# Pooled attention and a softplus feed-forward layer: other addresses for the tiles that TensorE reads

## The chip, the cores and the metric

The kernel runs on one core of a Trainium2 chip. The metric is the device time of one execution in microseconds (us), as the median of several runs. A profile, taken by the hardware profiler in one further execution, shows what each engine of the core did: PE is TensorE's matmuls, PEld its loads of the stationary operand, DVE is VectorE, ACT ScalarE, POOL GpSimd and SP the queue that issues the DMAs.

## The reference

Eight batches, eight heads, 576 positions, a head dimension of 64. Keys and values are averaged over groups of 8 positions, so there are 72 of each; the attention's result, as 4608 tokens of 512, goes through a feed-forward layer with 2048 inner columns and softplus between its two products.

```
k_p = k.reshape(B, H, 72, 8, D).mean(axis=3)
v_p = v.reshape(B, H, 72, 8, D).mean(axis=3)
scores = matmul(q, k_p.T) / sqrt(D);  scores -= max(scores)
attn = exp(scores) / (sum(exp(scores)) + 1e-9)
x = matmul(attn, v_p)                  # then to 4608 x 512
h = x @ w_in                           # 512 x 2048
g = maximum(h, 0) + log1p(exp(-abs(h)))
out = g @ w_out                        # 2048 x 512
```

## The kernel before, in words

The tokens are cut into 18 chunks of 256 (`CT`), each of two tiles of 128. For a chunk the kernel makes `x`, the attention's result with the 512 columns on the partitions, and then `h` in 16 blocks `f` of 128 inner columns, two blocks making a pair `u`. Each matrix is split into a high and a low part of float32r, and a product of two matrices is three products (high by high, low by high, high by low).

**First product** (`ffn1_products`, line 488): the stationary operand, which PE loads, is a 128x128 piece of the weights `w`; the moving operand, which PE streams past it, is a piece of `x` of 256 columns. A block `f` takes 12 matmuls, a pair 24.

**Second product.** In the first four chunks (lines 510 and 570) the stationary operand is a piece of `g` and the moving one a row of 512 weights, into `acc`. From the fifth chunk on (line 678, `pair2_fast`) a scheme of seven products on quarters takes the place of eight: the stationary operand is a 128x128 piece of `gh`, `gl` or of `so` (sums of pieces of g), and the moving one 256 columns of the weights, 21 matmuls a pair, into `m`. So `w` is the stationary operand on line 488 and the moving one on line 678.

**Attention** stands between these groups in short groups of its own on PE: `qTp` (transposes of q, line 331), `sc` (scores, 351), `ptp` and `ltp` (transposes of the normalised exponentials `pm` and `pe`, 414 and 426), `avp` (attention by values, 455 and 462) and `kT` (213). VectorE makes the lowest score `mn`, the sum `sm`, `pm`, `pe`, the low parts and the sums; ScalarE makes the exponentials, softplus and the high parts.

**What sets the order.** Every operation is given to a planner (`Order`) with a cost in us, the operations it follows and the kinds of tile slots it needs; the planner lists the operations by the start that it works out, and they are issued in that order. None of its costs, slots or kinds is touched.

**Where tiles lie.** A pool hands out addresses in SBUF (bytes within a partition) in the order in which its tags first appear, and pools lie one behind the other in the order in which they are opened: `const`, `wpool` (the weights, 16 tiles of 8192 bytes and what the early stretch uses for raw weights), then `one` (all else). The address modulo 256 bytes is called the phase here. All tiles that PE reads in the two products are multiples of 256 bytes long, so a tile's phase is set by what stands ahead of it in its pool and by the pools ahead of that, among them small tiles such as `mn` (32 bytes), `sm` (32 bytes) and `pe` (112 elements, of which 96 are used).

Of the kernel before, what the change touches and what calls it, by code (L numbers as in the profile page):

```python
# [9 lines left out]
F32 = mybir.dt.float32  # L10
F32R = mybir.dt.float32r
# [92 lines left out]
def pooled_attention_softplus_ffn(  # L104
# [11 lines left out]
    B, H, S, D = q.shape  # L116
    NTOK, DM = out.shape
    DFF = w_in.shape[1]
    P = 128
# [5 lines left out]
    CT = T * P  # L125
    HP = H // 2
# [3 lines left out]
    N1 = 3  # L130
# [4 lines left out]

    PSUM = bass.MemoryType.PSUM
    const = ctx.enter_context(tc.tile_pool(name="const", bufs=1))
    wpool = ctx.enter_context(tc.tile_pool(name="wpool", bufs=1))
    one = ctx.enter_context(tc.tile_pool(name="one", bufs=1))
    psum = ctx.enter_context(tc.tile_pool(name="psum", bufs=1, space=PSUM))  # L140
    dram = ctx.enter_context(tc.tile_pool(name="dram", bufs=1, space=bass.MemoryType.DRAM))
# [149 lines left out]
    R = 4 * KL  # L291
# [19 lines left out]
    def new_x(c, name=None):  # L311

        if c == N1 - 1:
            x_[c] = [one.tile([P, HP, CT], F32R, tag=tag, name="x") for tag in ("Sa", "Sb")]
        else:
            x = one.tile([P, 2, HP, CT], F32R, tag={"a": "X01", "b": "X23"}[name or "ab"[c % N1]],
                         name="x")
            x_[c] = [x[:, 0], x[:, 1]]

# [3 lines left out]
    class Tile:  # L323
# [30 lines left out]
        def least(self, j, ps, tag):  # L354

            if j == 0:
                self.mn = one.tile([P, 2, HP], F32, tag="mn" + tag, name="mn")
            nc.vector.tensor_reduce(out=self.mn[:, j], in_=self.view(ps), axis=AX.X, op=ALU.min)  # L358

        def view(self, ps):  # L360
# [9 lines left out]

        def exp_sum(self, j, ps, tag):
            if j == 0:
                self.sm = one.tile([P, H], F32, tag="sm" + tag, name="sm")
            for m in range(HP):
                h = 4 * (m // 2) + 2 * j + m % 2
                nc.scalar.activation(out=e_[self.c][:, self.t, h], in_=self.view(ps)[:, m],  # L376
                                     func=AF.Exp, scale=-1.0, bias=self.mn[:, j, m:m + 1],
                                     accum_out=self.sm[:, h:h + 1])

        def sum(self, tag):  # L380
            self.sm = one.tile([P, H], F32, tag="sm" + tag, name="sm")
            nc.vector.tensor_reduce(out=self.sm, in_=e_[self.c][:, self.t], axis=AX.X, op=ALU.add)

        def reciprocal(self):
# [7 lines left out]
                                    in1=self.sm.unsqueeze(2).to_broadcast([P, H, KM]), op=ALU.mult)  # L392

        def ends(self):

            pe = one.tile([P, 6 * R + 16], F32, tag="pe", name="pe")
            self.pe = pe[:, 0:6 * R].rearrange("p (a n r) -> p a n r", a=2, n=3)
            for a in range(2):
                hs = slice(4 * a, 4 * a + 4)
                nc.vector.tensor_tensor(  # L400
                    out=self.pe[:, a].rearrange("p n (h j) -> p n h j", h=4),
                    in0=e_[self.c][:, self.t, hs, KM:SP].unsqueeze(1).to_broadcast([P, 3, 4, KL]),
                    in1=self.sm[:, hs].unsqueeze(1).unsqueeze(3).to_broadcast([P, 3, 4, KL]),
                    op=ALU.mult)
# [61 lines left out]
    def av_high(c, r, ps, name=None):  # L466
        if c not in x_:
            new_x(c, name)
        nc.scalar.copy(out=x_[c][0][:, r::2], in_=ps.rearrange("p (g i) -> p g i", g=2))
# [475 lines left out]
    def attend(c):  # L945
# [17 lines left out]
        for t, x in enumerate(tiles):  # L963
# [7 lines left out]
            q_free[c, t] = o  # L971
            o = op(ACT, act(512), lambda x=x, s=s_q, n=s_qT: x.qT_out(s.tile, n.name), [o], [s_q, s_qT])
            ends, ss = [], [Slot("bank"), Slot("bank")]
            p = op(PE, 0.7, lambda x=x, ss=ss: x.scores([bank(s, "sc") for s in ss]), [o, *keys],
                   [s_qT, *ss])
            score_done.setdefault(c, []).append(p)
            for i, s in enumerate(ss):
                d = op(DVE, 0.46, lambda x=x, i=i, s=s, n=s_mn: x.least(i, s.tile, n.name), [p, *ends],
                       [s, s_mn])
                if c < N1:  # L980
                    def exp_sum(x=x, i=i, s=s, e=s_E[0], t=t, n=s_sm):
                        if c == 0 and 0 not in e_:
                            new_E(0)
                        e_[c] = e_[0]
                        x.slot = e.name
                        x.exp_sum(i, s.tile, n.name)
                    ends.append(op(ACT, 1.2, exp_sum, [d], [s, s_mn, s_sm, *s_E], table="exp"))
                else:
                    def less(x=x, i=i, s=s):
                        if c not in e_:  # L990
                            new_E(c)
                        x.less(i, s.tile)
                    ends.append(op(DVE, 0.46, less, [d, *e_free], [s, s_mn]))
            if c < N1:
                exps.extend(ends)
            else:
                subs += ends
            norms.append((x, ends, s_E, s_sm, s_pm, s_pe))
        if c == N1:
            ex = op(ACT, 1.2, lambda: exponential(e_[c]), subs, table="exp")  # L1000
# [403 lines left out]
```

## Time and profile before

| | us |
|---|---|
| median of three runs | 904.15 |
| lowest and highest | 903.52, 904.78 |
| the profiled execution | 903.13 |
| its span, first to last instruction | 901.4 |
| PE busy (98% of the span) | 883.9 |
| PEld busy (93%) | 840.9 |
| DVE busy (72%) | 648.7 |
| ACT busy (45%) | 407.5 |

The mean granted clock of TensorE is 0.999 of full speed. Of the chain of waits, followed back from the last instruction, 95% lies on PE: line 488 has 44% of the span, line 678 has 31%, the early second products 10%. In the profile's rows `m<-w,gh` means that the instruction writes m and reads w and gh; a piece of the chain is given with its start, its length and how many instructions of one line it joins. The pieces of the chain are worked out from starts and ends, so the length of a piece is the time until the next group of matmuls begins.

### The profile page before, as it was taken

The page shows a single profiled execution, that of the slowest core. Times are in us where ns is not written, and L with a number is a line of the kernel's source. Part 1 is how long each engine was busy: PE and PEld are TensorE (multiplying, and loading weights), DVE is VectorE, ACT ScalarE, POOL GpSimd, SP SyncE. Part 2 cuts the span into 40 slices and gives each one's busy share as a digit, 9 for nine tenths or more (in the row PEclk, how much of TensorE's full clock was granted, in tenths as well). Part 3 has the DMA queues.
Part 4 walks back from the last instruction along what each step waited for, and adds up shares of the span by engine and source line. Part 5 has one row for each costly group of instructions (what it writes and reads, how often), then busy time and mean ns, then how long its engine had stood idle before and what let it go on. Part 6 is the DMA issues. An engine that isn't in the chain of part 4 may idle for free.

```text
span 901.4 us, 20496 instructions
## 1 busy us (share of the span) xinstructions
PE 883.9 (98%) x8304; PEld 840.9 (93%) x8304; DVE 648.7 (72%) x1600; ACT 407.5 (45%) x824; POOL 2.4 (0%) x19
## 2 busy tenths in 40 slices
PE   5999999999999999999999999999999999999997
PEld 3689999889999999999999999999999999999997
DVE  5899999878767678787767666776576565657454
ACT  5864443354353534443444444353545353434332
POOL 1000000000000000000000000000000000000000
PEclk9999999999999999999999999999999999999999
DMA  9976544545997788787669765877566565656472
GB/s 233 312 227 202 173 162 158 161 153 200 299 267 240 231 239 245 214 249 228 227 200 261 217 227 168 257 239 228 193 179 228 177 222 187 212 162 225 163 241 76
DMA packets 107085, 191.12 MB, mean 212 GB/s; under 512 B 46064, under 2 KB 60400, under 8 KB 106992
## 3 DMA queue, kind: packets, MB, share of 16 engines
q1 hardware_dynamic: 106992, 189.82, 68.2%
q8 instruction: 65, 1.06, 0.5%
q14 instruction: 28, 0.23, 0.1%
HBM read 167.25 MB, written 22.54 MB: 211 GB/s over the span
## 4 chain that ended last, share of the span: by engine, by line
PE 95%; DVE 2%; DMA 1%; SPq 1%; ACT 1%; issue 0%; DVEq 0%; ACTq 0%
PE h L488 44%; PE m L678 31%; PE acc L510 7%; PE acc L570 3%; PE sc L351 2%; PE avp L455 2%; PE qTp L331 2%; PE ptp L414 2%; PE avp L462 1%; DMA wst<-in_moe_w_out_dram 1%; PE ltp L426 1%; DMA kvl<-in_v_dram 1%; ACT E L376 0%; SPq L302 0%; DVE o L699 0%
## 5 line engine op out<-in xcount | busy, mean ns | idle before, releaser
L488 PE MATMUL h<-x,w 128*128 128x256 f32 x3456 | 428.7, 280 | 0.2 <-ACT g L493 0.2
L488 PEld LDWEIGHTS h<-x,w 128*128 128x128 f32 x3456 | 413.3, 188 | 4.2 <-ACT g L493 0.6
L537 ACT ACTIVATE g<-h 128x512 f32<-128x512 f32 x120 | 71.9, 599 | 280.3 <-PE h L488 277.7
L678 PE MATMUL m<-w,so 128*128 128x256 f32 x1344 | 173.9, 278 | 0.0
L678 PEld LDWEIGHTS m<-w,so 128*128 128x128 f32 x1344 | 163.8, 188 | 0.0
L678 PE MATMUL m<-w,gh 128*128 128x256 f32 x672 | 131.6, 285 | 0.0
L588 DVE TENSOR_TENSOR sf<-g 128x128 f32<-128x128 f32 x112 | 32.7, 292 | 130.1 <-ACT g L537 129.6
L678 PEld LDWEIGHTS m<-w,gh 128*128 128x128 f32 x672 | 102.1, 188 | 1.7
L602 ACT CAST so<-sf 128x512 fp32r<-128x512 f32 x112 | 69.7, 622 | 58.1 <-DVE sf L591 57.6
L607 DVE TENSOR_TENSOR so<-sf,so 128x512 fp32r<-128x512 f32 x112 | 77.3, 690 | 22.8 <-ACT so L602 22.7
L678 PE MATMUL m<-w,gl 128*128 128x256 f32 x336 | 93.5, 278 | 0.0
L558 DVE TENSOR_TENSOR gl<-g,gh 128x384 fp32r<-128x384 f32 (+1 forms) x120 | 67.2, 560 | 0.5 <-ACT gh L551 0.3
L678 PEld LDWEIGHTS m<-w,gl 128*128 128x128 f32 x336 | 63.0, 188 | 0.0
L510 PE MATMUL acc<-w,g 128*128 128x512 f32 x192 | 60.1, 394 | 0.0
L551 ACT ACTIVATE gh<-h 128x384 fp32r<-128x384 f32 (+1 forms) x120 | 59.2, 493 | 0.0
L493 ACT ACTIVATE g<-h 128x256 fp32r<-128x256 f32 x96 | 32.1, 383 | 56.6 <-PE h L488 34.3
L699 DVE TENSOR_TENSOR o<-o,m 128x256 f32<-128x256 f32 x98 | 39.7, 417 | 3.5 <-ACT o L691 0.6
L510 PEld LDWEIGHTS acc<-w,g 128*128 128x128 f32 x192 | 33.5, 188 | 5.2
L510 PE MATMUL acc<-w,gl 128*128 128x512 f32 x96 | 37.9, 395 | 0.2 <-DVE gl L499 0.2
L591 DVE TENSOR_TENSOR sf<-g,sf 128x128 f32<-128x128 f32 x112 | 32.7, 292 | 3.9
L358 DVE TENSOR_REDUCE mn<-sc 128x4 f32<-128x288 f32 x72 | 31.3, 450 | 5.5 <-PE sc L351 5.4
L400 DVE TENSOR_TENSOR pe<-E,sm 128x96 f32<-128x96 f32 x72 | 15.2, 252 | 27.7 <-PE ltp L426 27.7
(165 smaller groups left out, 925.8 us busy)
## 6 DMA issues: line engine op xcount, KB each, us to landing
w<-wi SPq DMA_DIRECT2D x224, 512.0 KB
out_dram<-o SPq DMA_DIRECT2D x36, 256.0 KB
q<-in_q_dram SPq DMA_DIRECT2D x32, 256.0 KB
wst<-in_moe_w_in_dram SPq DMA_DIRECT2D x32, 256.0 KB
wst<-in_moe_w_out_dram SPq DMA_DIRECT2D x16, 512.0 KB
wi<-w SPq DMA_DIRECT2D x16, 512.0 KB
kst<-in_k_dram SPq DMA_DIRECT2D x24, 288.0 KB
vst<-in_v_dram SPq DMA_DIRECT2D x24, 256.0 KB
```

The source lines that it names most:

```text
L488: nc.tensor.matmul(out=ps[:, 0:CT], lhsT=row(w, kc), rhs=x[:, kc], start=first and kc == j == 0, stop=last and kc == KC - 1 and j == 2)
L493: nc.scalar.activation(out=g, in_=ps[:, 0:CT], func=AF.Softplus)
L510: nc.tensor.matmul(out=accs[c][t], lhsT=a[:, ts], rhs=w, start=f == 0 and j == 0, stop=f == FC - 1 and j == 2)
L537: nc.scalar.activation(out=g, in_=x.rearrange("p (b i) -> p b i", i=P), func=AF.Softplus)
L551: nc.scalar.activation(out=gh, in_=quarters(c, x.rearrange("p (b i) -> p b i", i=P)), func=AF.Softplus)
L558: nc.vector.tensor_tensor(out=gl, in0=quarters(c, g), in1=gh.bitcast(F32), op=ALU.subtract)
L588: tt(out=sf[:, 2], in0=g[:, 0], in1=g[:, 2], op=ALU.add)
L591: tt(out=sf[:, 3], in0=g[:, 3], in1=sf[:, 1], op=ALU.subtract)
L602: nc.scalar.copy(out=so[:, 0], in_=ss[c, u])
L607: nc.vector.tensor_tensor(out=so[:, 1], in0=sf, in1=so[:, 0].bitcast(F32), op=ALU.subtract)
L678: nc.tensor.matmul(out=ms[c][n], lhsT=x, rhs=y, start=u == 0 and j == 0 and n in (1, 6, 5, 4), stop=u == FP - 1 and j == 2 and n in (2, 7, ...
L699: nc.vector.tensor_tensor(out=o, in0=in0, in1=m[n], op=how)
```

## The change

Three pools are added. `x` of the chunks (but the third, c = 2, whose `x` has the tags `Sa` and `Sb` in `one`) goes into `xpool`, and `mn` into `mpool`; both are opened ahead of the weights' pool. `sm` goes into `spool`, between `wpool` and `one`. The tile `pe` loses its 16 unused elements (64 bytes).

```
+    xpool = ctx.enter_context(tc.tile_pool(name="xpool", bufs=1))
+    mpool = ctx.enter_context(tc.tile_pool(name="mpool", bufs=1))
     wpool = ctx.enter_context(tc.tile_pool(name="wpool", bufs=1))
+    spool = ctx.enter_context(tc.tile_pool(name="spool", bufs=1))
     one = ctx.enter_context(tc.tile_pool(name="one", bufs=1))
@@ new_x
-            x = one.tile([P, 2, HP, CT], F32R, tag={"a": "X01", "b": "X23"}[name or "ab"[c % N1]],
+            x = xpool.tile([P, 2, HP, CT], F32R, tag={"a": "X01", "b": "X23"}[name or "ab"[c % N1]],
                          name="x")
@@ least
-                self.mn = one.tile([P, 2, HP], F32, tag="mn" + tag, name="mn")
+                self.mn = mpool.tile([P, 2, HP], F32, tag="mn" + tag, name="mn")
@@ exp_sum
-                self.sm = one.tile([P, H], F32, tag="sm" + tag, name="sm")
+                self.sm = spool.tile([P, H], F32, tag="sm" + tag, name="sm")
@@ sum
-            self.sm = one.tile([P, H], F32, tag="sm" + tag, name="sm")
+            self.sm = spool.tile([P, H], F32, tag="sm" + tag, name="sm")
@@ ends
-            pe = one.tile([P, 6 * R + 16], F32, tag="pe", name="pe")
-            self.pe = pe[:, 0:6 * R].rearrange("p (a n r) -> p a n r", a=2, n=3)
+            self.pe = one.tile([P, 2, 3, R], F32, tag="pe", name="pe")
```

No instruction is added, removed or moved: on each of the five engines the instructions stand in the same order in both programs, with the same waits; only addresses differ. The phases (address modulo 256) of what PE reads, as the two programs lay the tiles out, are these:

| tile | before | after |
|---|---|---|
| `w`, the weights in all their slots | 192 | 0 |
| `x` (X01, X23) | 128 | 192 |
| `x` of c = 2 (Sa, Sb) | 128 | 64 |
| `g`, `gh`, `gl`, `so`, `pm` | 128 (slot G0 of `g`: 64) | 64 (G0 too) |
| `pe`, first and second half | 64, 192 | 192, 64 |
| `pT`, `lt_` | 128, 128 | 64, 64 |
| `q` and `qT` | 192 | 64 |
| `kT` (two tiles), `vs`, `vlo`, the identity | 192 and 64, 192, 192, 128 | the same |

As a difference, stationary minus moving modulo 256: on line 488 (`w` over `x`) it is 64 before and 64 after, but for c = 2, where it becomes -64; on lines 510, 570 and 678 (`g`, `gh`, `gl` or `so` over `w`) it is -64 before and 64 after. While the last matmul of a pair on line 488 streams `x`, the first piece of `g` is loaded for line 678: `g` minus `x` is 0 before and 128 after. From line 678 to line 488 the last matmul streams `w` and the next load is of `w`: 0 in both.

## Rows read from the trace of the kernel before

**Rows 1.** Busy time of each engine by stretch; PEclk is the granted clock.
```profile
242.00:897.00 655.00, 654.61 (x6391) 642.16 (x6389) 438.45 (x1194) 286.65 (x508) 0.00 (x0) 1.00 0.70 215
```

**Rows 2.** Chain of waits from 241 us and to 891 us: start, length, what.
```profile
241.33 2.75 PE h L488 x24
244.08 2.38 PE m L678 x21
246.46 2.83 PE h L488 x24
249.29 2.48 PE m L678 x21
...
881.21 2.47 PE m L678 x21
883.68 2.73 PE h L488 x24
886.41 2.38 PE m L678 x21
888.80 2.83 PE h L488 x24
```

**Rows 3.** Line 678's matmuls over `so`: ns min/median/max, first and last start.
```profile
L678 PE MATMUL m<-w,so x1344: 276/279/312, 244.6 to 896.0; 128*128 128x256 f32 x192
```

**Rows 4.** Chain of waits where attention stands between the products.
```profile
450.19 0.59 PE ptp L414 x4
450.77 2.47 PE m L678 x21
453.25 0.44 PE ptp L414 x4
453.69 2.75 PE h L488 x24
456.43 0.22 PE ltp L426 x2
456.65 2.48 PE m L678 x21
459.13 0.22 PE ltp L426 x2
459.35 2.83 PE h L488 x24
...
463.20 0.66 PE avp L462 x4
463.86 2.39 PE m L678 x21
466.25 0.87 PE qTp L331 x8
467.12 2.74 PE h L488 x24
469.86 0.66 PE sc L351 x32
470.52 2.58 PE m L678 x21
...
476.59 2.67 PE m L678 x21
```

**Rows 5.** Chain of waits: `kT` ahead of line 678, and a slow group behind `avp`.
```profile
279.50 2.52 PE m L678 x21
...
511.16 2.48 PE m L678 x21
```

**Rows 6.** Chain of waits in the early stretch, with the old second product.
```profile
204.87 2.75 PE acc L570 x12
...
211.01 2.80 PE acc L570 x12
```

**Rows 7.** Costliest groups: VectorE's work on `pe`; busy us, mean ns.
```profile
L400 DVE TENSOR_TENSOR pe<-E,sm 128x96 f32<-128x96 f32 x72 | 15.2, 252 | 27.7 <-PE ltp L426 27.7
```

## The prediction

> **What bounds the kernel now.** I read the busy time by stretch first. From 242 to 897 us PE works 654.61 of 655.00 us at a granted clock of 1.00, the upper level (2.4 GHz), while VectorE has 438 and ScalarE 287 us of work [rows 1]. In that stretch nothing can be won by making anybody wait less: the time is the number of matmuls by the time from one to the next. What lies before it ends in the same work, and what lies behind it is a tail of 4.4 us that VectorE sets.
>
> So the second view is the chain of waits, piece by piece. The pieces of one kind are not equally long, though they hold the same instructions on tiles of the same shape: a pair on line 488 (24 matmuls) takes 2.73 to 2.75 us or 2.83, a group on line 678 (21 matmuls) 2.38 or 2.47 to 2.48 [rows 2]. By matmul that is 2.73/24 = 113.8 ns against 117.9, and 2.38/21 = 113.3 against 117.6. I call the two rhythms fast and slow. The clock isn't the cause, since they alternate every few microseconds at a clock of 1.00, nor a wait, since PE is never idle. The matmul itself reads 276 to 279 ns with an upper end of 312 [rows 3]; matmuls overlap, and the rhythm shows in the pieces.
>
> Then I counted the pieces from 241 to 897 us, 110 pairs of line 488 and 110 groups of line 678 (the first and last of each kind are in [rows 2]; a group behind `sc` is 0.20 us longer in either rhythm, 2.58 and 2.67 in [rows 4]). Of line 488, 57 are fast and 53 slow, of line 678, 48 and 62. Which one a group has follows from what stands ahead of it:
> - from line 488 straight to 678 the rhythm stays (57 times of 57);
> - from line 678 straight to 488 it flips (71 of 71), so that two pairs of groups run fast, slow, slow, fast [rows 2];
> - behind `ptp` line 488 is fast in 12 of 13 cases and line 678 slow in 7 of 7; behind `qTp` line 488 is fast in 11 of 11; behind `ltp` line 488 is slow in 11 of 13 and line 678 in 9 of 9; `avp` leaves line 678 fast 5 times and slow 7; `sc` leaves the rhythm as it was; both groups behind `kT` are slow [rows 4, 5].
>
> A rhythm that is set by what went before and then lasts, at the same clock and with no wait, must hang on where in some cycle of the memory's or PE's own the two streams of reads meet. What differs between the lines is whether the stationary operand's address stands 64 bytes ahead of the moving one's (line 488) or 64 behind (line 678). That is the quantity that the change alters, and no trace of before shows line 678 at any other.
>
> **The change part by part.** Nothing is added, removed or moved on any engine, so every term is a change of rhythm or nothing. The prices: a slow pair of line 488 costs 2.83 - 2.73 = 0.10 us more than a fast one, a slow group of line 678 2.47 - 2.38 = 0.09 [rows 2]. If all became fast it would save 53 x 0.10 + 62 x 0.09 = 10.9 us; if all became slow, cost 57 x 0.10 + 48 x 0.09 = 10.0 us. These are the two ends for the stretch of the fast scheme.
>
> 1. Line 678 with its stationary operand 64 ahead. It then stands to its moving operand as line 488 does today. I take line 488's behaviour for it, in two respects. First, the flip from line 678 to 488 comes about because the rhythm's place is shifted by the one sign in line 678 and back by the other in line 488; with the same sign in both a direct boundary keeps the rhythm. Second, behind `ptp` and `qTp` line 678 becomes fast as line 488 is (23 of 24); behind `ltp`, `avp` and `kT` I leave each group what it is. Following the 220 groups in order under these rules, slow are: 11 pairs and 9 groups behind `ltp`, 7 groups behind `avp`, 2 behind `kT`, and those that run on from them without interruption (5 pairs and 4 groups directly, one of each over `sc`). That makes 17 pairs and 23 groups, where there are 53 and 62: saved (53 - 17) x 0.10 + (62 - 23) x 0.09 = 3.6 + 3.5 = 7.1 us. The ends are the two of above. I choose this value between them since it uses line 488's outcomes, the nearest rows. If only the flip goes and the groups behind `ptp` and `qTp` stay what they are, the same count gives 23 and 36, so 5.3 us; if `ltp` too leaves line 678 fast, up to 9.8.
>
> 2. The boundary from 488 to 678, where `g` stands 128 from `x` instead of at 0. I count nothing, since one matmul in 24 is concerned and it is no part of a steady stream; below it is the slower rival.
>
> 3. The early second product (lines 510 and 570), 3 x 16 x 2 x 3 + 8 x 2 x 2 x 3 = 384 matmuls of 512 columns, in 32 pieces of 12. They show 2.75 and 2.80 us [rows 6], so 32 x 0.05 = 1.6 us at most either way; I take 0, since their rows do not tell which of them the address makes.
>
> 4. `x` of c = 2, now 64 ahead of the weights: 16 x 12 = 192 matmuls, 8 pairs. At the price of a pair this is 0.8 us either way. The early stretch has its pairs nearly all fast, so if anything it loses; I take 0.
>
> 5. `pe` without its unused elements, `mn` and `sm` in pools of their own, `pm`, `q`, `pT` and `lt_` at other phases. VectorE's instruction on `pe` reads and writes the same 96 elements, 252 ns in 72 instructions [rows 7]; were each a third longer that would be 72 x 0.08 = 6 us on an engine that is idle for 655 - 438 = 217 us of the long stretch [rows 1], so it is hidden. If the cover were gone it would be those 6 us. PE's short groups come to some 5 us a chunk (those of [rows 4], with a second `sc` of 0.66 and the other part of `avp`), and there are 14 chunks; a change of rhythm of the size above (4%) would be 14 x 0.2 = 2.8 us either way at most, and I take 0.
>
> The sum is -7.1 us. Against the profiled execution that is 903.13 - 7.1 = 896.0; the median stands 1.0 us above that execution, so the forecast is 904.15 - 7.1 = 897.0 us.
>
> Of a rule that speaks against this: the Trainium skill, "SBUF — State Buffer", section "Who interferes with whom", gives PE two read ports, one for the moving operand and one for the loads of the stationary one, independent of each other, and says that "PE and ACT never wait on anyone". By that rule addresses can't matter and the sum would be 0 (rival two). The trace doesn't agree with it as it stands: the same instruction has two rhythms, 113.3 and 117.6 ns, with no other engine's work to tell them apart. But it doesn't show that the address is what decides, either.
>
> **The rivals.**
> - The flip stays at one of the two boundaries. If line 678's boundary with 488 keeps its rhythm but the new 128 between `x` and `g` makes the other one flip, the alternation goes on with the places exchanged. Counted in order this leaves 45 slow pairs and 59 slow groups, so -1.1 us; with line 678 fast behind `ptp` and `qTp`, 53 and 57, so -0.5 us. The time is 903.0 to 903.7: no change. For it: flips are the rule in before, and which boundary makes them is inferred from one arrangement. Against it: it needs the single matmul at a boundary to decide, not the 21 or 24 of the group.
> - Addresses don't decide; the rhythm is set by the lengths of what stands between the groups, which don't change. Then the time is 904.15. For it: `sc` and `kT` shift the place too. Against it: a flip at one kind of boundary 71 times of 71 and at the other never.
> - Slower: the slow rhythm takes over. The two boundaries are now both of one sort for the streams but 128 apart for `g` and `x`, so that each time line 678 begins it falls into the slow rhythm. From the point where 488 hands over to 678 directly: with line 678 slow and 488 keeping that rhythm, 84 pairs and 95 groups are slow, +6.1 us, 910.2; where some direct pairs still come back, 64 and 85, +3.2 us, 907.3; with all slow 914.1. It decides as soon as more than 115 of the 220 are slow, weighed by nearly equal prices. For it: slow is already the commoner rhythm in line 678, and `ltp` makes it the rule; with no flip there is nothing that brings a slow run back to fast before the next interruption. Against it: behind `ptp` and `qTp` line 488 at 64 ahead nearly always settles fast, and in each chunk there are three or four of them.
>
> **How the numbers follow.** A difference under 0.2%, 1.8 us, can't be told from none here. The forecast's own case (5 to 10 us saved, 894 to 899) has 0.53, a smaller gain of 2 to 5 us in which some of the interruptions come out slow 0.03: faster 0.56. The two cases without a difference, with the unknown terms 3 and 4 about them, have 0.12 and 0.09: same 0.21. The slower rival has 0.23. The range that holds 8 in 10 takes in the first case with the early terms' 2.4 us below it (10.9 saved and a little more gives 892), the cases of no change, and the slower one to +3.9 (908); what is left out is mainly its upper part. The likeliest case's own range is 892 to 899.
>
> **What would show it.** Right: in the changed kernel's chain of waits, runs of pieces 2.73, 2.38, 2.73, 2.38 with no alternation, groups of line 678 behind `ptp` at 2.38, and about 40 slow pieces in place of 115; the span shorter by 7 us, nearly all of it between 242 and 897 us, with PE's busy share and the clock as before. Step 1 is wrong if flips remain (then look at which boundary has them) or if the groups behind `ptp` stay at 2.47. Step 2 is wrong if the boundary from 488 to 678 shows a change of rhythm. Steps 3 and 4 show in the stretch before 242 us, in pieces of 12 other than 2.75 and in pairs of the third chunk at 2.83. The prediction fails altogether if pieces have a third length, which no row of before has.

## The result and the profile after

| | before, us | after, us |
|---|---|---|
| median of nine runs | 904.61 | 907.53 |
| lowest and highest | 902.65, 906.08 | 905.32, 907.99 |
| profiled execution, span | 903.13, 901.4 | 906.08, 904.3 |
| PE busy | 883.9 | 886.5 |

The changed kernel is slower by 0.3%: the ratio to before is 1.003 with a 95% interval of 1.0017 to 1.0042. A second timing of the same kernel gave 1.0029 (1.0017 to 1.0040). The forecast was 897.0 us, 0.8% faster, with 892 to 908 as the range; the median lies in the range, and the sign is wrong.

In the changed kernel lines 488 and 678 are 490 and 680, and lines 510 and 570 are 512 and 572. The row by stretch answers to [rows 1]: PE is as full as it was, at the same granted clock, only later done.

```profile
242.00:897.00 655.00, 654.79 (x6381) 642.18 (x6380) 437.29 (x1190) 287.56 (x509) 0.00 (x0) 1.00 0.71 216
```

The chain of waits, shortly behind 242 us and near the end (start, length, what), answers to [rows 2]. At first there is something like the old alternation; then it stops, and what remains is line 490 always fast (2.74) and line 680 always slow (2.47).

```profile
243.09 2.83 PE h L490 x24
245.92 2.39 PE m L680 x21
248.31 2.83 PE h L490 x24
251.15 2.48 PE m L680 x21
253.62 2.74 PE h L490 x24
256.36 2.47 PE m L680 x21
...
876.19 2.74 PE h L490 x24
878.93 2.47 PE m L680 x21
881.41 2.74 PE h L490 x24
884.15 2.47 PE m L680 x21
886.62 2.74 PE h L490 x24
889.36 2.47 PE m L680 x21
```

A pair of groups (one of line 490, one of 680) takes 2.74 + 2.47 = 5.21 us in this pattern. In the old alternation two such pairs took 2.73 + 2.38 + 2.83 + 2.47 = 10.41, or 5.21 each. So the pattern that replaces the old one costs just what that did. The count says the same: of the 220 groups behind 242 us 45 of line 490 and 70 of line 680 are slow, 115 together, as many as before; the prediction expected about 40.

Where attention stands between the products (answers to [rows 4, 5]), line 680 now is fast behind `sc` (2.60, where before it was 2.58 or 2.67) and at times behind `ptp`; line 490 is slow behind `ptp` half the time:

```profile
452.88 0.59 PE ptp L416 x4
453.47 2.43 PE m L680 x21
455.89 0.44 PE ptp L416 x4
456.33 2.83 PE h L490 x24
459.16 0.22 PE ltp L428 x2
459.38 2.48 PE m L680 x21
461.86 0.22 PE ltp L428 x2
462.08 2.83 PE h L490 x24
...
465.93 0.68 PE avp L464 x4
466.61 2.40 PE m L680 x21
469.00 0.87 PE qTp L335 x8
469.88 2.74 PE h L490 x24
472.61 0.66 PE sc L355 x32
473.27 2.60 PE m L680 x21
```

In the early stretch the old second product is longer (answers to [rows 6]): a piece of 12 matmuls that took 2.75 us takes 2.79, with nothing standing in between (the 2.80 of [rows 6] was a piece behind `ptp`).

```profile
206.37 2.79 PE acc L572 x12
...
212.65 2.81 PE acc L572 x12
```

The work on `pe` (answers to [rows 7]) and the matmuls over `so` (answers to [rows 3]) tell nothing new: 252 ns as before, and a median of 281 ns for 279, which follows the slower rhythm.

**Where the 3 us are.** I took from both traces the time from each group's first matmul to the next group's first, and summed the differences by kind and stretch (us, against the first profile of before). "Late" is all behind 242 us, "early" 62 to 242, "start" what lies ahead of that, where PE waits for transfers. (The chain's pieces run from the end of one group's last matmul to the end of the next group's last, so behind an interruption the two differ: the pair that starts at 453.44 us in before takes 2.83 us here and 2.75 in [rows 4].)

| | start | early: acc | early: line 490 | late: line 490 | late: line 680 | late, all |
|---|---|---|---|---|---|---|
| before, second profile | 1.6 | 0.0 | 0.0 | 0.4 | 0.2 | 1.0 |
| after | -0.2 | 1.0 | 1.0 | -0.4 | 1.5 | 1.3 |
| after, second profile | 1.5 | 1.0 | 1.0 | -0.6 | 1.1 | 0.9 |
| g_m64 | 3.4 | -0.1 | -0.1 | -0.5 | 0.6 | 0.1 |
| x_p64 | 1.0 | 1.1 | 2.1 | 0.6 | -1.2 | -0.4 |
| kk_0 | 2.1 | 0.1 | 1.7 | 4.8 | 3.6 | 8.1 |
| a_id | -0.7 | 1.0 | 0.8 | -1.2 | 0.3 | -0.8 |

The start differs by up to 2 us between two profiles of the same kernel, so it is no part of the explanation. The late stretch of the kernel before differs by 1.0 us as well, where I had expected a repeat within 0.3. That isn't the clock: the second profile's mean is 0.995 for 0.999, but in it the granted clock is below 1.00 only at the start.

```profile
0.00:62.00 62.00, 50.82 (x578) 37.26 (x579) 45.71 (x93) 41.63 (x147) 2.36 (x19) 0.94 0.92 260
242.00:897.00 655.00, 654.62 (x6384) 641.94 (x6383) 437.45 (x1191) 287.35 (x509) 0.00 (x0) 1.00 0.72 216
```

Most of it, 0.8 us, is a single place near 620 us, around a wait of `sc` for VectorE. The first profile of after has such a place near 277 us (0.4 us), the second one near 623 us (0.35 us). Without them the late stretch reads 0.9 and 0.6 us for after, 0 and 0.2 for before. The early columns repeat within 0.1.

So there are two losses: 2.0 us early, half in the old second product and half in the pairs behind it, and a smaller one late, of 0.4 to 0.9 us. Late, the direct handovers lose: line 680 directly behind 490 (56 groups in either trace) sums to 138.4 us where it was 135.9, and line 490 directly behind 680 (71 groups) to 197.6 where it was 198.8; this makes +1.3, in the second profile of after too. The groups behind an interruption give part of it back: line 680 takes 1.4 us less there (the single place left out), line 490 0.5 to 0.7 us more.

The tallies of groups behind 242 us, F for fast and S for slow, "F to S" for a group that is slow behind a fast one:

| | before | after | g_m64 | x_p64 | kk_0 | a_id |
|---|---|---|---|---|---|---|
| 490 to 680: F to F, F to S | 30, 0 | 0, 41 | 30, 0 | 0, 30 | 0, 0 | 0, 42 |
| 490 to 680: S to S, S to F | 26, 0 | 14, 1 | 26, 0 | 0, 26 | 56, 0 | 13, 1 |
| 680 to 490: F to F, F to S | 0, 41 | 0, 24 | 0, 40 | 42, 0 | 0, 0 | 0, 24 |
| 680 to 490: S to S, S to F | 0, 30 | 0, 47 | 1, 30 | 29, 0 | 71, 0 | 0, 47 |
| 490 behind ptp: F, S | 12, 1 | 6, 7 | 8, 5 | 0, 13 | 3, 10 | 7, 6 |
| 490 behind ltp: F, S | 2, 11 | 1, 12 | 11, 2 | 2, 11 | 0, 13 | 10, 3 |
| 680 behind ltp: F, S | 0, 9 | 6, 3 | 0, 9 | 3, 6 | 0, 9 | 9, 0 |
| 680 behind avp: F, S | 6, 7 | 6, 7 | 1, 12 | 13, 0 | 1, 12 | 13, 0 |
| 680 behind sc: F, S | 12, 10 | 22, 0 | 12, 10 | 22, 0 | 0, 22 | 21, 1 |

The last handover from 490 to 680, behind which two groups of 680 stand together, is left out: 56 of the prediction's 57 remain. Second profiles of before and after gave the same numbers but for one or two groups in a row. The pattern belongs to the layout, not to chance in a run.

### The profile page after: what moved, and what is told of

It reads as the page before. It is cut to its first block, busy times and chain, and to the rows that moved or that the text cites. A ratio compares the mean times of both kernels' runs of the same rounds, so it can differ in the third digit from the quotient of the medians.

```text
span 904.3 us, 20496 instructions
## 1 busy us (share of the span) xinstructions
PE 886.5 (98%) x8304; PEld 842.2 (93%) x8304; DVE 648.8 (72%) x1600; ACT 407.9 (45%) x824; POOL 2.4 (0%) x19
## 4 chain that ended last, share of the span: by engine, by line
PE 93%; DMA 3%; DVE 2%; SPq 1%; ACT 1%; issue 0%; DVEq 0%; ACTq 0%
PE h L490 44%; PE m L680 30%; PE acc L512 7%; PE acc L572 3%; PE sc L355 2%; PE avp L457 2%; PE qTp L335 2%; PE ptp L416 1%; PE avp L464 1%; DMA vst<-in_v_dram 1%; DMA q<-in_q_dram 1%; PE ltp L428 1%; DMA kvl<-in_v_dram 1%; SPq L864 0%; ACT E L380 0%; PE kvlp L877 0%
```

## The experiments

Places are given as bytes from the weights' phase, modulo 256: in before x is at -64 and g at -64, in after x at -64 and g at +64. All kernels have the same instructions in the same order; only pads and pools differ. Line numbers are those of the changed kernel, shifted by up to three where a pad's lines were added. Theory A was that g's place against the weights makes the loss; rivals were the place of x against g at the handover (B) and places in absolute terms or against the constants (C).

### g back to -64, x where the change put it (g_m64)

```
-                self.sm = spool.tile([P, H], F32, tag="sm" + tag, name="sm")
+                self.sm = spool.tile([P, 24], F32, tag="sm" + tag, name="sm")[:, 0:H]
```

> The changed kernel with 128 bytes more between the weights and the other tiles: g stands 64 behind the weights again (and x of the third chunk too), x and the weights stay where the change put them. Theory A (what counts is g's phase against the weights', which the second product reads together): pieces of 12 early second products at 2.75 us again (after: 2.80), line 680's groups alternating 2.38 and 2.47, time about 904.6, 0.997 of the changed kernel. Rival B (x against g where line 490 hands over to 680: 0 before, 128 after, 0 here): the same time, so it is not told apart here but by x_p64. Rival C (where tiles lie absolutely, x ahead of the weights, or the attention's operands against the constants): 907.5 as the changed kernel, no alternation.

904.41 us; against the kernel before 0.9994 (0.9982 to 1.0006). The chain has the old alternation and the old 2.75:

```profile
208.13 2.75 PE acc L572 x12
...
879.23 2.47 PE m L680 x21
881.70 2.73 PE h L490 x24
884.44 2.38 PE m L680 x21
886.82 2.83 PE h L490 x24
```

So moving x ahead of the weights, the new pools and the missing pad cost nothing that can be told here: the loss hangs on 128 bytes in the place of `one`. With g that moves all else in `one` (`q`, `pm`, `pT`, x of the third chunk); the length of the early acc pieces goes with g's place against the weights in every kernel at 64 ahead or behind.

### x at +64, g at +64 (x_p64)

```
-                self.mn = mpool.tile([P, 2, HP], F32, tag="mn" + tag, name="mn")
+                self.mn = mpool.tile([P, 24], F32, tag="mn" + tag, name="mn")[:, 0:8].rearrange("p (j m) -> p j m", j=2)
```

> The changed kernel with 128 bytes more between x and the weights: x 64 ahead of the weights, g still 64 ahead, so x and g have one phase again, as before. Theory A: the second product as in the changed kernel, acc pieces 2.80 and line 680 at 2.47 to 2.48 behind line 490; line 490 with its sign changed may alter by itself; 907 or more. Rival B (the boundary): alternation of 2.38 and 2.47 back, early acc 2.75, about 904.6.

906.89 us; 1.0020 (1.0009 to 1.0031). Both theories had a part: the early pieces stay long, as A says, and the alternation is back, as B says.

```profile
208.60 2.80 PE acc L572 x12
...
876.95 2.83 PE h L490 x24
879.78 2.39 PE m L680 x21
882.17 2.72 PE h L490 x24
884.90 2.48 PE m L680 x21
```

The rows show more than either expected. It is not the old alternation: here the rhythm turns at the handover from 490 to 680 (slow 2.83, then fast 2.39) and stays at the one from 680 to 490, in before it was the other way round. And it is slower than before though it alternates, by its early stretch (+3.2 us in the table's two columns); behind 242 us it has 104 slow groups of 220 and is no slower than before.

### g at 0 and at 128 (g_0, g_128)

```
(g_0: the pool of sm ahead of x)          (g_128: sm tiles of 16 elements, of which 8 are used)
```

> g and the sums at the weights' own phase (0), x 64 behind as in the changed kernel. Theory A has no number for this phase, but a test: the early acc pieces and line 680 must go together, acc at 2.75 with line 680 at times 2.38, acc at 2.80 with line 680 steadily 2.47; as 0 lies between -64 and 64, between 904.6 and 907.5. Rival B (x against g, here 64): also between, but with acc pieces unchanged at 2.75, since x has no part in them.

> g and the sums 128 from the weights' phase, x 64 behind as in the changed kernel. Theory A: a third place, so acc and line 680 at other lengths than in both kernels; before, the one slot of g that stood at this phase had acc matmuls longer than its neighbours, so 907.5 to 912. Rival B (x against g 192 here): no change of acc, 904.6 to 907.5.

909.96 us, 1.0058 (1.0042 to 1.0074), and 910.59 us, 1.0062 (1.0044 to 1.0081). Both have line 680 at a third length, 2.50, behind line 490 always, as here in g_0:

```profile
208.05 2.72 PE acc L572 x12
...
885.11 2.74 PE h L490 x24
887.85 2.50 PE m L680 x21
```

The time of g_0 lies above the ranges of both theories. The test I had set for theory A failed: in g_0 early pieces run at 2.72 (227 ns a matmul, the shortest of all kernels) while line 680 is steadily slow, at 2.50. In g_128 theory A's range holds, and acc too has another length (2.77). So the products of 512 and of 256 columns don't go together. For rival B the same kernel is against it, since acc did change.

### x at +64, g at -64 (kk_0, kk_64, kk_128)

From the tallies I had by then a rule, theory F: a handover turns the rhythm when the line that begins has its stationary operand 64 ahead of its moving one, and keeps it when 64 behind. (For line 490 the stationary operand is the weights, so x at -64 is "ahead".) The opposite of the changed kernel should then have no turns at all. kk_64 and kk_128 shift everything from x on by 64 and 128 bytes against the identity.

```
-    kT = [const.tile([P, HP, SP], F32, name=f"kT{i}") for i in range(2)]
+    kT = [pool.tile([P, HP, SP], F32, name=f"kT{i}") for i, pool in enumerate((mpool, spool))]
+    pad = ppool.tile([P, 16], F32, name="pad")      (kk_64: ppool ahead of xpool; kk_128: 32 elements)
```

> One tile of the pooled keys moved between x and the weights, the other between the weights and the rest (128 bytes modulo 256 each): x 64 ahead of the weights, g 64 behind them, the other way round than in the changed kernel; the identity at the weights' phase. Theory F (flips: from line 680 to 490 the rhythm flips where x is behind the weights and stays where it is ahead; from 490 to 680 it flips where g is ahead and stays where it is behind): no flips at direct boundaries at all, runs of one rhythm from one interruption to the next; early second products at 2.75 us per 12; since x_p64 and g_m64 have nearly every group behind ptp, qTp and ltp slow, about 190 of 220 slow and 910 to 913 us. Rival G (each line's rhythm is its own, whatever stands ahead): alternation or 2.48 behind 2.74 as in the kernels so far, 904 to 907.

> As kk_0, but all from x on lies 64 bytes further, so that the identity (the moving operand of the transposes) stands 64 behind the weights, as in the kernel before. Theory F with interruptions that the identity decides: behind ptp and qTp line 490 is fast again in most cases, these runs last, 893 to 899 us. Theory F with interruptions that x's own place decides: slow as kk_0, 910 to 913. Rival G: 904 to 907.

> As kk_0, but all from x on lies 128 bytes further, the identity 128 from the weights as in the changed kernel. Theory F with the identity deciding: line 490 fast behind qTp, mixed behind ptp, 895 to 903. With x's own place deciding: 910 to 913. Rival G: 904 to 907.

913.66, 913.41 and 913.03 us; 1.0104 (1.0089 to 1.0118), 1.0104 (1.0088 to 1.0120), 1.0099 (1.0083 to 1.0115). There is no turn at any of 127 handovers in any of the three, and 202 to 211 of 220 groups are slow, as theory F with x's own place deciding had it (its 910 to 913 us was a little short):

```profile
887.76 2.47 PE m L680 x21
890.24 2.83 PE h L490 x24
```

All these handovers go from slow to slow; the few fast groups each stand ahead of an interruption. The hope of kk_64, that the identity's old place would make the runs fast, fell.

### The changed kernel with the identity at its old place (a_id64, a_id), and second profiles

a_id64 puts x at -64 and g at +64 as the change does, but the identity 64 behind the weights as in before and the values as far from their moving operand as in before; a_id puts the identity back and leaves the values where the changed kernel has them. Both move the two tiles of the keys `kT`.

```
-    kT = [const.tile([P, HP, SP], F32, name=f"kT{i}") for i in range(2)]
+    kT = [pool.tile([P, HP, SP], F32, name=f"kT{i}") for i, pool in enumerate((kpool, const))]
+    pad = const.tile([P, 16], F32, name="pad")      (a_id; a_id64: in a pool ahead of xpool. kpool behind one)
```

> The changed kernel's x (64 behind) and g (64 ahead), but the identity and the values at the places against the weights that they have in the kernel before (all from x on 64 further, one tile of the pooled keys at the very end). If g alone makes the loss, as the changed kernel: acc pieces 2.80, line 680 at 2.47 behind line 490, 906.5 to 908. If the attention's operands against the constants make a part of it: early acc as there, but line 490 fast behind ptp again, and 905 to 906.5.

> The kernel before, profiled a second time. If the tallies of fast and slow groups belong to the layout, they repeat: line 490's forerunner (488) fast behind ptp and qTp, slow behind ltp, within one or two groups of the first profile, and the stretch behind 242 us within 0.3 us. If they hang on chance in the run (where the transfers of the start end), they differ by several groups, and the 1 us that the late stretch of the changed kernel loses can't be laid to the layout.

> The changed kernel again. By the layout: early second products 2.80 us per 12, late stretch 1 us over the kernel before, ltp followed by slow groups of line 490, ratio 1.002 to 1.004. By chance in the run: early part the same, late stretch elsewhere.

> a_id64 again. By the layout: both groups behind ltp fast as in its first profile, late stretch 1 us under the kernel before, early part 1.7 us over it, ratio 0.999 to 1.001. By chance: 1.002 to 1.004 as the changed kernel.

> a_id64 with 64 bytes between the keys and the values, so that the identity stands to the weights as in the kernel before, and the values to their moving operand as in the changed kernel. If the identity decides the rhythm behind the transposes, groups behind ltp are fast as in a_id64 and the ratio is 0.999 to 1.001; if the values do, slow as in the changed kernel and 1.002 to 1.004. By chance: no order in it.

a_id64 took 903.83 us, 0.9997 (0.9987 to 1.0007), and the second time 904.46, 0.9994 (0.9981 to 1.0006); a_id 904.81, 1.0000 (0.9987 to 1.0013); the changed kernel beside them 906.78, 1.0029 (1.0017 to 1.0040). The two timings of a_id64 lie below both ranges that its first text gave, and line 490 behind `ptp` didn't become fast again (8 of 13, where before has 12). The early loss is there in all of them (+1.8 in a_id), the handovers have the changed kernel's tallies, and what differs is the groups behind `ltp` and `avp`: in a_id fast 10 of 13 (line 490's) and 9 of 9 (line 680's) behind `ltp`, 13 of 13 behind `avp`.

```profile
412.39 0.22 PE ltp L430 x2
412.61 2.74 PE h L492 x24
415.35 1.02 PE avp L459 x16
416.37 0.67 PE avp L466 x4
417.04 2.40 PE m L682 x21
```

and in the changed kernel at the same place:

```profile
413.97 0.22 PE ltp L428 x2
414.19 2.83 PE h L490 x24
417.02 1.02 PE avp L457 x16
418.04 0.68 PE avp L464 x4
418.72 2.49 PE m L680 x21
```

a_id moved the identity and the keys `kT` but left the values where the changed kernel has them, and is as fast as a_id64; so it isn't the values. Whether the identity alone does it, or `kT` has a part, these runs don't separate. Against the changed kernel this saves some 2 us late (904.81 for 906.78 us; 97 slow groups of 220 for 115), which is as much as the early loss.

### x and g both at -32, -96, +32 and +96 (xg_m32, xg_m96, xg_p32, xg_p96)

Pads of 32 to 96 bytes between the pools.

> Places between those tried: x and g both 32 bytes behind the weights. Line 490 then has its stationary operand 32 ahead of the moving one, line 680 32 behind. Theory L (only the 64-byte line counts): each line behaves as at 0 or at 64, so line 680 at 2.38/2.48 or at 2.50, 904 to 912 us. Theory S (every step counts): rhythms between, with m groups of another length than 2.38, 2.48 and 2.50, anywhere from 895 to 915.

> x and g both 96 bytes behind the weights. Theory L: as at -64 or at 128, so 904 to 912 us with known lengths of groups. Theory S: other lengths, 895 to 915.

> x and g both 32 bytes ahead of the weights. Theory L: as at 0 or at 64: flips from line 490 to 680 and none back, as in x_p64, or line 680 steadily at 2.50; 906 to 912 us. Theory S: other lengths, 895 to 915.

> x and g both 96 bytes ahead of the weights. Theory L: as at 64 or at 128, 906 to 912 us. Theory S: other lengths, 895 to 915.

916.41, 920.90, 915.36 and 924.58 us; 1.0122 (1.0086 to 1.0158), 1.0175 (1.0134 to 1.0216), 1.0109 (1.0077 to 1.0142) and 1.0213 (1.0179 to 1.0247). Theory L is out: there are new lengths, 2.80 to 2.88 for line 490 and 2.45 to 2.52 for line 680 at direct handovers, and no group of these is left at the fast 2.73 or 2.38. Theory S had the new lengths, but all four times lie above its 895 to 915. The slowest is xg_p96:

```profile
894.52 2.88 PE h L492 x24
897.40 2.50 PE m L682 x21
```

No layout tried beats the kernel before. a_id, a_id64 and g_m64 equal it. The pads also move the identity and the attention's tiles, so these four don't separate the part of x and g.

## Why the prediction was wrong

**The bound and the lever were right.** PE's full stretch, the two rhythms at one clock, and that addresses set them: the runs differ in nothing but addresses and reach from 903.8 to 924.6 us. The rival by which addresses don't matter is out.

**Step 1 failed, in its first respect.** It said that with the same sign in both lines a direct boundary keeps the rhythm, since the two signs cancelled in before. With 64 ahead in both, neither boundary kept it: from 680 to 490 the rhythm turns 71 times of 71, as it did before, and from 490 to 680 all 41 fast groups turn slow. So there are 115 slow groups where the sum had 40. What the runs show in its place is that the line that begins counts: with its stationary operand 64 ahead of the moving one it turns the rhythm, with 64 behind it keeps it. In before line 488 is 64 ahead and turns 71 times of 71, line 678 is behind and keeps 56 of 56; in x_p64, with the signs exchanged, line 680 turns 56 of 56 and line 490 keeps 71 of 71. I had read the flip as a sum of both lines' signs, from one layout in which the rule "the line that begins decides" would have fitted as well. kk_0, with 64 behind in both and no turn in 127, fits either reading; x_p64 and the changed kernel tell them apart.

The rule has an exception that I can't explain. In the changed kernel 14 of the 15 slow groups of line 490 are followed by a slow group of 680, where the rule wants a fast one, and 13 of 14 in a_id. In both g stands 128 from x, as the slower rival had it; in x_p64, where g and x have one phase, slow turns fast 26 times of 26. So the place of x against g may have a part of its own, which no run here separates from the rest.

The mistake goes further, since "no turns" was to be the gain. The kernels without turns are the slowest at steps of 64 bytes (913.0 to 913.7 us): with 64 behind, what starts after an interruption mostly starts slow, and then nothing turns it back. The two signs trade one for the other. With 64 ahead line 490 starts fast behind `ptp`, `qTp` and `ltp` 25 times of 37 in before and 17 in the changed kernel, and turns at handovers; with 64 behind it does so twice in x_p64 and 4 times in kk_0, and keeps. Both steady patterns with turns cost 5.21 us a pair of groups, and none of the four combinations of signs that ran had the 7.1 us of the sum.

**Step 1, second respect: partly right.** Line 680 did take over line 488's habit of starting fast: behind `sc` 22 of 22, behind `ltp` 6 of 9, behind `ptp` and `qTp` 4 of 8 where I had said all. But line 490 behind `ptp` fell from 12 of 13 to 6 of 13. The identity, too, had moved against the weights (from 64 behind to 128); putting it back with `kT` didn't restore that (7 of 13 in a_id), but made the groups behind `ltp` and `avp` fast. I had written such places off under step 5 with 0 and bounds of 2.8 us; a_id puts the worth of the identity and `kT` at some 2 us, through the rhythm of the groups behind, not in the short groups themselves.

**Step 2 was wrong by its own sign**: the boundary from 490 to 680 changes the rhythm now (42 times of 56). It doesn't need the 128 between g and x for that, since in x_p64, with the two at one phase, it does so 56 times of 56. The slower rival built on this step came nearest: line 680 does begin slow nearly each time 490 hands over (55 of 56). It erred where it let line 490 keep that rhythm; 490 turns back fast 47 times of 47, so the handovers cost 1.3 us in place of 6.1. That its middle figure, 907.3 us, is next to the measured 907.5 is luck: it has all of its +3.2 us late, and 2.0 of the measured loss lie early.

**Steps 3 and 4 were mis-sized at 0.** The early second product costs 1.0 us of the 1.6 that I had as its bound: a piece was 2.75 undisturbed in before and is 2.79 now. And early pairs of line 490 cost 1.0 us. I had priced only the third chunk's x (0.8 at most); by the groups of the trace that chunk has 0.3, and the other chunks, whose x didn't move against the weights, have the rest: directly behind the second product, now at its other rhythm, their matmuls often run at 117.8 ns where they ran at 114.4. That they take this from the second product is my reading; g_m64, where both are gone, has g back in its place and doesn't separate them.

**What stays open.** The rules above are counted, not derived: the prediction argued that the rhythm hangs on where two streams of reads meet in some cycle, and no run here shows that, nor what else makes the two rhythms. Why moving the identity and `kT` changes the rhythm behind `ltp` is open too.

## What to carry to other kernels

Where PE is full at one clock and pieces of the same instructions have two lengths, tally them by what stands ahead of them and by the phases of both operands; layouts alone spread this kernel over 2.3%, all of it on the slow side of the kernel before, and a layout is tested by one pad, not by an argument. A rule inferred from one layout that fits by two readings should be tried with each reading before it is summed over a hundred groups. A pad moves everything behind it: list every operand that shifts against another, the small transposes' identity too.

## What the hardware showed that I had not expected

- The four layouts with x and g an odd multiple of 32 bytes from the weights were slower (915.4 to 924.6 us) than all at multiples of 64 (at most 913.7): line 490 at 2.80 to 2.88 us for 24 where 2.73 and 2.83 are the lengths at 64.
- Early matmuls of 512 columns run at 227 ns with stationary and moving operand at one phase, 229 at -64 and some 233 at +64, while a group of line 680, of 256 columns a matmul, takes 2.50 us at one phase, more than at -64 or +64 in either rhythm.
- The same layout repeats its pattern of some 220 groups from run to run to within a few groups, while the runs of one kernel differ by 3 us. Between its two profiles 1.6 us of that lie in the start, where the second has a granted clock of 0.94 up to 62 us, and 1.0 us late at a clock of 1.00.
